# Values of one attention unit and scores of the next in one TensorE burst

## The chip, the cores and the metric

The kernel runs on one core of a Trainium2 chip. The metric is device time in microseconds (us). Three runs of the kernel before took 1695.42, 1698.11 and 1698.41 us; the median is 1698.11.

## The reference

Three steps follow each other; everything is float32.

```
q_c, k_c, v_c = chunks of 64 positions of q, k, v         # 8 x 8 heads, 576 positions, head size 64
scores = (q_c @ k_c^T) / 8
attn   = exp(scores - rowmax); attn = attn / (rowsum + 1e-9)
x      = attn @ v_c                                       # rows: 4608 tokens, columns: 512
h = x @ w_in;   g = h if h > 0 else exp(min(h, 0)) - 1;                        x = g @ w_out
h = x @ w_in2;  g = h if h >= 1, 0 if h <= -1, else (h + 1)^2 / 4;             out = g @ w_out2
```

Both pairs of weights are 512 x 2048 and 2048 x 512.

## The kernel before

Tokens are cut into 9 blocks of 512. A block is made of 4 attention units of 128 tokens, so there are 36 units; a unit is two chunks of 64 tokens for 8 heads. Each factor of the large products is split into a rounded high part and the rest, and three products (high by high, rest by high, high by rest) are added, so a layer of one block takes 16 steps of 12 matmuls into the hidden layer (L603, tile `h`) and 12 out of it (L633, tiles `acc`), all 128 x 512. The steps of the first layer run in the order: block 0's first 7, all of block 1, block 0's other 9, then blocks 2 to 8. What block 0 has summed after its first 7 steps is put aside in DRAM (`part`), loaded again (L845) and added at the end (L867). The second layer, from about 925 us on, has a product scheme of its own (L689, L787) and no attention.

A unit goes through the engines like this. TensorE: scores (`scores`, L429, 16 matmuls of 64 x 64 in the four quarters of the array, tile `s`). VectorE: row maximum (`top`, L443) and subtraction (`sub`, L448). ScalarE: exponential (`exp`, L454). VectorE: sums, guard, reciprocal, product (`total`, `guard`, `invert`, `norm`, L459 to L469). TensorE: four 128 x 128 transposes (`turn`, L474). ScalarE: copy to SBUF (`turned`, L479). TensorE: values (`values`, L481, again 16 matmuls of 64 x 64). ScalarE and VectorE: high part and rest of the result, the x of the first layer (`high`, L499; `low`, L503). From unit 4 on, `s`, the transposes and the values' result `o` take turns in one pair of banks, `a`, which serves one of them at a time.

The order of all instructions is written out by a planner (`Plan`, L37). Every piece of work is an `Op` with an engine (P TensorE, V VectorE, A ScalarE, S the DMA queue of SyncE, X none), a cost, events that it waits for, buffers that it takes and gives. The planner always takes the one that could start first, with a small share of its rank, and so fixes the place of each instruction in its engine's queue; an engine then works strictly in that order. A generator `unit` (L414) yields the Ops of one unit. Buffers that matter: `acc` 2 pairs of banks, `a` 1, `m` 7 slots in SBUF for weights of the second layer on their way to DRAM, for `part` and for results. A unit's x can be written only when the block that used the buffer before is through its hidden layer (`x_free`, L946).

Meanwhile the weights of the second layer are loaded, converted (L194 to L218, L336 to L345), split (L298, L301) and stored (`w3s`, `w4s`, L305).

Of the kernel before, what the change touches and what calls it, by code (L numbers as in the profile page):

```python
# [16 lines left out]
P = 128  # L17
# [86 lines left out]
def chunk_attention_moe_moe2(ctx, tc, qk, v, w1, w2, w3, w4, out):  # L104
# [13 lines left out]
    CH = 64  # L118
# [3 lines left out]
    UPB = BLK // P  # L122
    NU = NT // P
# [22 lines left out]
    T = {}  # L146
# [16 lines left out]
    def pair(tag, i, name):  # L163

        return ps(tag, i, [P, 2, BLK], name)
# [222 lines left out]

    KF = NF - UPB

    def first_loads():
        for g in range(UPB):
            T["qk", g] = wp.tile([P, 2, 4, 2, CH], F32, tag=f"w0_{KF + g}", name=f"qk_{g}")
            if g % 2 == 0:
                v2 = wp.tile([P, 2, 2, 4, D], F32, tag=f"w1_{KF + g // 2}", name=f"v_{g}")
            T["v", g] = v2[:, g % 2]

        def load_qk():
            for i in range(2):
                nc.sync.dma_start(out=T["qk", g][:, i], in_=qk[g, i])  # L400

        def load_v():
            nc.sync.dma_start(out=T["v", g], in_=v[g])

        for i in range(UPB + 1):
            if i < UPB:
                g = i
                yield Op("S", 1.2, load_qk, after=[], event=("qk", g), move=1.46)
            if i >= 1:
                g = i - 1  # L410
                yield Op("S", 0.6, load_v, after=[], event=("v", g), move=0.73)
        yield Op("X", 0.0, lambda: None, after=[], event="weights")

    def unit(u, pool):  # L414
        b, j = divmod(u, UPB)
# [11 lines left out]
            return slice(r * CH, (r + 1) * CH)  # L427

        def scores(i, _):  # L429
            s = T["s", u] = pair(pool, i, ("s2", u))[:, :, :4 * CH].rearrange("p r (t j) -> p r t j", t=4)  # L430
            q, k = T["qk", u][:, 0], T["qk", u][:, 1]
            for t in range(4):
                for r in range(2):
                    for c in range(2):
                        nc.tensor.matmul(  # L435
                            s[half(c), r, t, :], lhsT=q[half(r), t, c, :], rhs=k[half(r), t, c, :],
                            start=True, stop=True,
                        )
# [6 lines left out]
        def sub(i):  # L445

            p = sb("p", i, [P, 4, 2, CH], F32, ("p", u))
            nc.vector.tensor_tensor(  # L448
                out=p.rearrange("p t r j -> p r t j"), in0=T["s", u],
                in1=T["mx", u].to_broadcast([P, 2, 4, CH]), op=ALU.subtract,  # L450
            )
# [28 lines left out]

        def values(i):  # L481

            o = T["o", u] = pair(pool, i, ("o2", u))[:, :, :2 * P].rearrange("p r (s i) -> p r s i", s=2)
            pt, vt = T["pt", u], T["v", u]
            for s in range(2):
                for ch in range(2):
# [21 lines left out]
        if u >= UPB:  # L508
            yield Op("S", 0.6, load_qk, after=before("scores", "q"), event=("qk", u), move=1.46)
            yield Op("S", 0.6, load_v, after=before("values", "v"), event=("v", u), move=0.73)  # L510
        hold = {}

        def scores2(i, k):
            hold["s"], hold["p"] = i, k
            scores(i, k)

        yield Op("P", 1.0, scores2, after=[("qk", u)], take=(pool, "p"), event=("scores", u), late=0.06)
        yield Op("V", 0.6, top)
        yield Op("V", 0.6, lambda: sub(hold["p"]), give=[(pool, hold["s"])])
        yield Op("A", 0.52, exp)  # L520
        yield Op("V", 0.6, total)
        yield Op("V", 0.07, guard)
        yield Op("V", 0.09, invert)
        yield Op("V", 0.6, norm, late=0.1)
        ti, pi = yield Op("P", 0.44, turn, take=(pool, "pt"), give=[("p", hold["p"])], late=0.06)
        yield Op("A", 0.48, lambda: turned(pi), give=[(pool, ti)], event=("pt", u), late=0.1)
        (oi,) = yield Op(
            "P", 1.0, values, after=[("pt", u), ("v", u)] + x_free(b), take=(pool,), give=[("pt", pi)],
            event=("values", u), late=0.06,
# [509 lines left out]
```

## Time and profile before

| | before |
|---|---|
| median of 3 runs | 1698.11 us |
| the profiled execution | 1695.53 us |
| its span | 1693.7 us |
| TensorE busy | 1656.3 us (98%) |
| VectorE busy | 907.2 us (54%) |
| ScalarE busy | 761.8 us (45%) |
| mean granted TensorE clock | 0.993 |

The profiled execution is one of its own, 2.6 us under the median; the span is from its first to its last instruction. PE is TensorE, PEld its weight loads, DVE VectorE, ACT ScalarE, SP SyncE with the DMA queue. Names such as `h<-xh,w` say which tile is written from which. A matmul's length in a row is from its start to its result, and matmuls overlap: twelve of some 0.40 us each follow each other in 2.8 us. What one costs the stream is therefore read from the distance of starts. A 64 x 64 matmul of float32 shows as two records, so a burst of 16 is x32; transposes show as one record each.

### The profile page before, as it was taken

How to read it: one execution, taken by the hardware profiler on the slowest of the kernel's cores; microseconds unless marked ns; L12 is line 12 of the kernel's file. 1: busy time of each engine (PE TensorE's matmuls, PEld its weight loads, DVE VectorE, ACT ScalarE, POOL GpSimd, SP SyncE). 2: the span in 40 equal slices, each digit the busy share in tenths (PEclk: the TensorE clock that was granted, in tenths of full speed). 3: DMA queues.
4: the chain of work that ended last, by engine and by line, in shares of the span. 5: the costliest groups of instructions: out<-in, count | busy, mean ns of one | idle time of the engine just before them, and what ended most of it. 6: DMA issues, size and time to landing. Idle time of an engine off the chain costs nothing.

```text
span 1693.7 us, 26194 instructions
## 1 busy us (share of the span) xinstructions
PE 1656.3 (98%) x10658; PEld 1392.1 (82%) x10658; DVE 907.2 (54%) x1521; ACT 761.8 (45%) x1416; POOL 0.7 (0%) x6
## 2 busy tenths in 40 slices
PE   5999998999999999999999999999999999999998
PEld 4778776777777787778787888888888888888887
DVE  7993455465555645555324464645454545454544
ACT  6883444454444545454433343434343434343433
POOL 0000000000000000000000000000000000000000
PEclk7999999999999999999999999999999999999999
DMA  8640235243332514333355233333333333333332
GB/s 286 204 132 20 63 96 164 71 144 90 110 123 80 172 56 134 94 117 112 107 185 193 100 131 119 127 119 124 120 124 120 125 119 128 119 130 112 112 112 100
DMA packets 105272, 207.23 MB, mean 122 GB/s; under 512 B 8896, under 2 KB 48832, under 8 KB 105152
## 3 DMA queue, kind: packets, MB, share of 16 engines
q1 hardware_dynamic: 105152, 205.56, 36.7%
q8 instruction: 84, 1.38, 0.4%
q14 instruction: 36, 0.29, 0.1%
HBM read 162.53 MB, written 42.99 MB: 121 GB/s over the span
## 4 chain that ended last, share of the span: by engine, by line
PE 87%; DVE 6%; ACT 2%; DMA 1%; issue 0%; SPq 0%; DVEq 0%; ACTq 0%
PE acc L633 23%; PE h L603 21%; PE h L787 11%; PE acc L787 11%; PE acc L689 10%; PE a L689 9%; DVE xu L564 2%; PE a L490 1%; PE a L435 1%; PE a L474 1%; DVE m L218 0%; ACT gh L745 0%; DVE gh L751 0%; DVE t L736 0%; DVE gh L755 0%
## 5 line engine op out<-in xcount | busy, mean ns | idle before, releaser
L633 PE MATMUL acc<-gh,w 128*128 128x512 f32 x1152 | 302.9, 401 | 0.6 <-ACT m L863 0.5
L603 PE MATMUL h<-xh,w 128*128 128x512 f32 x1152 | 293.5, 397 | 1.3 <-DVE t L618 1.3
L603 PEld LDWEIGHTS h<-xh,w 128*128 128x128 f32 x1152 | 217.1, 189 | 53.5 <-DVE t L618 3.0
L633 PEld LDWEIGHTS acc<-gh,w 128*128 128x128 f32 x1152 | 214.0, 189 | 50.7 <-ACT m L863 1.5
L689 PEld LDWEIGHTS a<-xu,w 128*128 128x128 f32 x1512 | 198.8, 188 | 16.4 <-ACT a L721 3.6
L689 PEld LDWEIGHTS acc<-xu,w 128*128 128x128 f32 x1512 | 199.6, 188 | 12.5
L689 PE MATMUL a<-xu,w 128*128 128x256 f32 x1512 | 204.0, 282 | 0.1
L689 PE MATMUL acc<-xu,w 128*128 128x256 f32 x1512 | 203.2, 282 | 0.0
L624 DVE TENSOR_TENSOR gl<-t,gh 128x512 fp32r<-128x512 f32 x144 | 99.1, 688 | 185.7 <-PE acc L633 155.9
L633 PE MATMUL acc<-gl,w 128*128 128x512 f32 x576 | 166.2, 402 | 0.0
L610 ACT ACTIVATE t<-h 128x512 f32<-128x512 f32 x144 | 85.8, 596 | 174.2 <-DVE gl L624 149.4
L618 DVE SCALAR_TENSOR_TENSOR t<-t,h 128x512 f32<-128x512 f32 x144 | 98.7, 685 | 115.4 <-ACT t L614 114.3
L603 PE MATMUL h<-xl,w 128*128 128x512 f32 x576 | 157.3, 395 | 0.0
L603 PEld LDWEIGHTS h<-xl,w 128*128 128x128 f32 x576 | 108.5, 188 | 25.5
L633 PEld LDWEIGHTS acc<-gl,w 128*128 128x128 f32 x576 | 105.3, 189 | 23.2
L621 ACT ACTIVATE gh<-t 128x512 fp32r<-128x512 f32 x144 | 89.9, 625 | 63.5 <-PE acc L633 62.9
L787 PE MATMUL acc<-w,t 128*128 128x512 f32 x432 | 112.7, 397 | 0.4 <-ACT t L759 0.4
L787 PE MATMUL acc<-w,v 128*128 128x512 f32 x432 | 111.7, 394 | 1.4 <-ACT v L759 1.4
L787 PE MATMUL h<-w,p 128*128 128x512 f32 x432 | 112.3, 395 | 0.0
L614 ACT ACTIVATE t<-t 128x512 f32<-128x512 f32 x144 | 90.9, 631 | 4.0
L736 DVE TENSOR_TENSOR t<-acc,z 128x512 f32<-128x512 f32 x36 | 24.9, 691 | 126.2 <-PE acc L689 126.2
L787 PEld LDWEIGHTS acc<-w,v 128*128 128x128 f32 x432 | 76.2, 188 | 14.3 <-ACT v L759 1.6
(99 smaller groups left out, 1772.7 us busy)
## 6 DMA issues: line engine op xcount, KB each, us to landing
w<-w4s SPq DMA_DIRECT2D x144, 512.0 KB, 4.2
raw<-w SPq DMA_DIRECT2D x32, 512.0 KB, 6.4
qk<-qk SPq DMA_DIRECT2D x32, 512.0 KB, 4.0
m<-w SPq DMA_DIRECT2D x64, 256.0 KB, 4.0
w<-w3s SPq DMA_DIRECT2D x28, 512.0 KB, 3.6
w3s<-m SPq DMA_DIRECT2D x48, 256.0 KB, 2.8
v<-v SPq DMA_DIRECT2D x36, 256.0 KB, 2.9
x<-m SPq DMA_DIRECT2D x36, 256.0 KB, 2.9
```

Source lines behind the costliest of these rows:

```text
L435: nc.tensor.matmul(s[half(c), r, t, :], lhsT=q[half(r), t, c, :], rhs=k[half(r), t, c, :], start=True, stop=True,)
L564: nc.vector.tensor_sub(place(j), T[src], T["xh", b, n])
L603: nc.tensor.matmul(h, lhsT=w[:, wi, c, :], rhs=x[:, c, :], start=n == 0, stop=n == 3 * NC_ - 1)
L610: nc.scalar.activation(sb("t", i, [P, BLK], F32, ("act", s)), T["h", s], AF.Relu, scale=-1.0)
L614: nc.scalar.activation(t, t, AF.Exp, scale=-1.0)
L618: nc.vector.scalar_tensor_tensor(out=t, in0=t, scalar=-1.0, in1=T["h", s], op0=ALU.add, op1=ALU.max)
L621: nc.scalar.activation(sb("gh", i, [P, BLK], F32R, ("gh", s)), T["act", s], AF.Copy)
L624: nc.vector.tensor_sub(sb("gl", gi, [P, BLK], F32R, ("gl", s)), T["act", s], T["gh", s])
L633: nc.tensor.matmul(T["acc", 0, b, m], lhsT=w[:, wi, m, :], rhs=T[g, s], start=first and (wi, g) == (0, "gh"), stop=last and g == "gl",)
L689: nc.tensor.matmul(quarter(q), lhsT=w[:, wi, c, :], rhs=x[:, c, :], start=start and k == 0, stop=clean and k == 5, skip_group_check=True,)
L736: nc.vector.tensor_tensor(out=h, in0=halves(hold["h"])[:, 2:4], in1=hold["z"].to_broadcast([P, 2, HB]), op=ALU.add)
L787: nc.tensor.matmul(T["acc", 1, b, 2 * side + k], lhsT=g[:, j, k * P:(k + 1) * P], rhs=w[:, wi], start=(i, j, wi, lo) == (0, 0, 0, False), ...
```

## The change

From the third block on (units 8 and later) a unit's values are no longer an Op of their own: the scores of the next unit take the pair of banks `a`, and its first half of each bank is for the scores, the second half for the values of the unit before, which are issued right ahead of the scores. The copy and the rest of these values (`high`, `low`) are yielded by the next unit too, between its subtraction and its exponential. The pair of banks is given back when both are through. Values lie in the second half of the banks in all units. The planner's cost of scores without values is 0.65 instead of 1.0, of scores with values 1.3.

```diff
+    MERGE = 2 * UPB
         def scores(i, _):
-            s = T["s", u] = pair(pool, i, ("s2", u))[:, :, :4 * CH].rearrange("p r (t j) -> p r t j", t=4)
+            two = T["two", u] if u > MERGE else pair(pool, i, ("s2", u))
+            s = T["s", u] = two[:, :, :4 * CH].rearrange("p r (t j) -> p r t j", t=4)
         def values(i):
-            o = T["o", u] = pair(pool, i, ("o2", u))[:, :, :2 * P].rearrange("p r (s i) -> p r s i", s=2)
+            two = pair(pool, i, ("o2", u))
+            if u >= MERGE:
+                T["two", u + 1] = two
+            o = T["o", u] = two[:, :, 2 * P:].rearrange("p r (s i) -> p r s i", s=2)
...
+        T["unit", u] = values, high, low
+        after = u > MERGE
         def scores2(i, k):
             hold["s"], hold["p"] = i, k
+            if after:
+                T["unit", u - 1][0](i)
             scores(i, k)
-        yield Op("P", 1.0, scores2, after=[("qk", u)], take=(pool, "p"), event=("scores", u), late=0.06)
+        ready, give = [("qk", u)], []
+        if after:
+            ready += [("pt", u - 1), ("v", u - 1)] + x_free((u - 1) // UPB)
+            yield Op("X", 0.0, lambda: None, after=ready)
+            give = [("pt", T["ptslot", u - 1])]
+        yield Op(
+            "P", 1.3 if after else 0.65, scores2, after=ready, take=(pool, "p"), give=give, event=("scores", u), late=0.06
+        )
+        if after:
+            yield Op("X", 0.0, lambda: None, event=("values", u - 1))
         yield Op("V", 0.6, top)
-        yield Op("V", 0.6, lambda: sub(hold["p"]), give=[(pool, hold["s"])])
-        yield Op("A", 0.52, exp)
+        yield Op("V", 0.6, lambda: sub(hold["p"]), give=[] if after else [(pool, hold["s"])], event=("sub", u))
+        if after:
+            yield Op("A", 0.48, T["unit", u - 1][1], after=[("scores", u)], event=("xh", u - 1))
+            yield Op("V", 0.6, T["unit", u - 1][2], after=[("sub", u), ("xh", u - 1)], give=[(pool, hold["s"])], event=("x", u - 1))
+        yield Op("A", 0.52, exp, after=[("sub", u)])
...
+        if MERGE <= u < NU - 1:
+            T["ptslot", u] = pi
+            return
```

TensorE's order around the values of unit 11, before and after. `pt` is a unit's transposed weights, `p` the same before the transposes, `a` the pair of banks.

```order
203 L474 MATMUL a_2072<-ident,p_1983 128x128 x4
204 L633 MATMUL acc_1948<-gl_2013,w_9_1102 128x512 x2
205 L633 MATMUL acc_1949<-gl_2013,w_9_1102 128x512 x2
206 L603 MATMUL h_2083<-xh_241,w_13_1328 128x512 x8
207 L603 MATMUL h_2083<-xl_242,w_13_1328 128x512 x4
208 L633 MATMUL acc_1948<-gh_2056,w_10_1178 128x512 x4
209 L633 MATMUL acc_1949<-gh_2056,w_10_1178 128x512 x4
210 L490 MATMUL a_2112<-pt_2081,v_75 64x64 x16
211 L633 MATMUL acc_1948<-gl_2058,w_10_1178 128x512 x2
212 L633 MATMUL acc_1949<-gl_2058,w_10_1178 128x512 x2
```

In the changed kernel (its lines stand some 2 to 27 further down: L438 is scores, L477 transposes, L496 values, L630 and L660 the large matmuls):

```order
197 L477 MATMUL a_2035<-ident,p_1990 128x128 x4
198 L660 MATMUL acc_1999<-gh_1967,w_8_1036 128x512 x4
199 L660 MATMUL acc_2000<-gh_1967,w_8_1036 128x512 x4
200 L496 MATMUL a_2055<-pt_2048,v_75 64x64 x16
201 L438 MATMUL a_2055<-qk_72 64x64 x16
202 L660 MATMUL acc_1999<-gl_1987,w_8_1036 128x512 x2
203 L660 MATMUL acc_2000<-gl_1987,w_8_1036 128x512 x2
204 L630 MATMUL h_2098<-xh_236,w_13_1334 128x512 x8
205 L630 MATMUL h_2098<-xl_237,w_13_1334 128x512 x4
```

The scores of unit 12 now follow the values of unit 11 at once, into the same `a`; before, they came 24 large matmuls after them. There are 27 such places. Counted in the whole order, 32 to 72 large matmuls, mostly 40 or more, then lie between a burst and the transposes of its unit, except for units 14 (12) and 15 (24).

TensorE at the end of block 0, where the transposes of unit 14 (row 261 before, 260 after) stand ahead of the first output matmuls of block 2 (row 263 in both). Before:

```order
252 L490 MATMUL a_2407<-pt_2405,v_75 64x64 x16
253 L603 MATMUL h_2428<-xh_1729,w_3_550 128x512 x8
254 L603 MATMUL h_2428<-xl_1730,w_3_550 128x512 x4
255 L435 MATMUL a_2444<-qk_72 64x64 x16
256 L603 MATMUL h_2468<-xh_1729,w_4_610 128x512 x8
257 L603 MATMUL h_2468<-xl_1730,w_4_610 128x512 x4
258 L435 MATMUL a_2497<-qk_73 64x64 x16
259 L603 MATMUL h_2521<-xh_1729,w_5_684 128x512 x8
260 L603 MATMUL h_2521<-xl_1730,w_5_684 128x512 x4
261 L474 MATMUL a_2559<-ident,p_2490 128x128 x4
262 L490 MATMUL a_2572<-pt_2567,v_74 64x64 x16
263 L633 MATMUL acc_2595<-gh_2372,w_0_352 128x512 x4
```

After:

```order
254 L660 MATMUL acc_2000<-gh_2337,w_15_1457 128x512 x2
255 L660 MATMUL acc_2000<-gl_2354,w_15_1457 128x512
256 L496 MATMUL a_2454<-pt_2380,v_75 64x64 x16
257 L438 MATMUL a_2454<-qk_72 64x64 x16
258 L630 MATMUL h_2506<-xh_1718,w_5_725 128x512 x8
259 L630 MATMUL h_2506<-xl_1719,w_5_725 128x512 x4
260 L477 MATMUL a_2538<-ident,p_2519 128x128 x4
261 L496 MATMUL a_2547<-pt_2543,v_74 64x64 x16
262 L438 MATMUL a_2547<-qk_73 64x64 x16
263 L660 MATMUL acc_2581<-gh_2382,w_0_371 128x512 x4
```

Two of the three groups of hidden matmuls have moved ahead of block 0's last output matmuls, and the scores of unit 15 have moved behind the transposes of unit 14. VectorE at the same place: the adds of the partial sums (`m<-acc,m`, L867 before, L894 after), the softmax of unit 14 (`p_2490` before, `p_2519` after) and weights of the second layer (L345, L301). Before:

```order
317 L867 TENSOR_TENSOR m_2514<-acc_1948,m_2514 128x512
318 L345 TENSOR_TENSOR m_2539<-m_2539,m_2267 128x256
319 L867 TENSOR_TENSOR m_2518<-acc_1948,m_2518 128x512
320 L867 TENSOR_TENSOR m_2534<-acc_1949,m_2534 128x512
321 L345 TENSOR_TENSOR m_2485<-m_2267,m_2485 128x256
322 L465 RECIPROCAL sm<-sm 128x8
323 L345 TENSOR_TENSOR m_2540<-m_2267,m_2539 128x256
324 L469 TENSOR_TENSOR p_2490<-p_2490,sm 128x512
325 L448 TENSOR_TENSOR p_2556<-a_2497,mx 128x2x4x64
```

After:

```order
316 L446 TENSOR_REDUCE mx<-a_2454 128x8
317 L645 SCALAR_TENSOR_TENSOR t_2494<-t_2494,h_2384 128x512
318 L451 TENSOR_TENSOR p_2519<-a_2454,mx 128x2x4x64
319 L509 TENSOR_TENSOR xl_2328<-a_2454,xh_2327 128x4x128
320 L462 TENSOR_REDUCE sm<-p_2519 128x8
321 L465 TENSOR_SCALAR sm<-sm 128x8
322 L468 RECIPROCAL sm<-sm 128x8
323 L894 TENSOR_TENSOR m_2504<-acc_2000,m_2504 128x512
324 L472 TENSOR_TENSOR p_2519<-p_2519,sm 128x512
325 L301 TENSOR_TENSOR m_2436<-m_2436,m_2534 128x512
326 L894 TENSOR_TENSOR m_2526<-acc_2000,m_2526 128x512
```

Here the third add stands right ahead of the normalising of unit 14 and the fourth behind it; the first two come directly before these rows. On SyncE's queue the load for the third add now comes behind the load of the next `v`, which waits for unit 13's values, and behind the stores of the first two sums; that for the fourth comes behind a further store of weights and a load of `qk`.

ScalarE around the values of unit 12, with the engines that an instruction waits for. Before:

```order
238 L198 ACTIVATE m_2267<-m_2264,bit_bias 128x256
239 L610 ACTIVATE t_2275<-h_2237 128x512 [waits DVE_49,PE_49]
240 L614 ACTIVATE t_2275<-t_2275 128x512 [waits Activation_49]
241 L499 ACTIVATE xh_2301<-a_2280 128x4x128 [waits PE_49]
242 L621 ACTIVATE gh_2319<-t_2222 128x512
243 L610 ACTIVATE t_2331<-h_2306 128x512 [waits DVE_49,PE_49]
```

After:

```order
238 L648 ACTIVATE gh_2273<-t_2192 128x512 [waits PE_49]
239 L637 ACTIVATE t_2318<-h_2213 128x512 [waits DVE_49]
240 L641 ACTIVATE t_2318<-t_2318 128x512 [waits Activation_49]
241 L505 ACTIVATE xh_2327<-a_2275 128x4x128 [waits DVE_49,PE_49]
242 L457 ACTIVATE p_2325<-p_2325 128x512
243 L648 ACTIVATE gh_2337<-t_2230 128x512 [waits PE_49]
```

The copy of the values (`xh`) now waits for VectorE as well as TensorE, and the exponential of the next unit (L457) stands right behind it.

## Rows read from the trace of the kernel before

**Rows 1.** The page, parts 1 and 4: busy time; the chain by engine
```profile
PE 1656.3 (98%) x10658; PEld 1392.1 (82%) x10658; DVE 907.2 (54%) x1521; ACT 761.8 (45%) x1416; POOL 0.7 (0%) x6
...
PE 87%; DVE 6%; ACT 2%; DMA 1%; issue 0%; SPq 0%; DVEq 0%; ACTq 0%
```

**Rows 2.** Stages: stretch, length, busy us (instructions) by engine, granted clock, DMA
```profile
0.00:90.00 90.00, 69.19 (x742) 54.38 (x743) 80.90 (x157) 67.09 (x115) 0.70 (x6) 0.91 0.69 234
90.00:250.00 160.00, 159.47 (x1068) 126.31 (x1068) 87.48 (x152) 81.23 (x141) 0.00 (x0) 1.00 0.24 74
250.00:270.00 20.00, 14.51 (x139) 10.74 (x139) 12.62 (x28) 6.55 (x12) 0.00 (x0) 0.83 0.64 203
270.00:800.00 530.00, 528.72 (x3469) 421.26 (x3462) 290.09 (x520) 265.74 (x499) 0.00 (x0) 1.00 0.35 111
...
915.00:935.00 20.00, 17.20 (x91) 14.32 (x90) 7.16 (x11) 5.45 (x11) 0.00 (x0) 1.00 0.50 158
```

**Rows 3.** Chain of waits, 236 to 275: start, length, what
```profile
236.10 0.62 PE a L435 x32
...
237.86 2.78 PE h L603 x12
...
252.61 4.08 DMA m<-part
```

**Rows 4.** TensorE's timeline around a scores burst: start, length, line, tiles, count
```profile
584.33 1.08 PE L633 MATMUL acc<-gl,w 128*128 128x512 f32 x4
585.33 0.69 PE L435 MATMUL a<-qk 64*64 64x64 f32 x32
585.96 2.13 PE L633 MATMUL acc<-gh,w 128*128 128x512 f32 x8
587.92 1.10 PE L633 MATMUL acc<-gl,w 128*128 128x512 f32 x4
```

**Rows 5.** Inside a values burst: two looks, from the second and the last group
```profile
562.92 0.41 PE L490 MATMUL a<-pt,v 64*64 64x64 f32 x16
...
563.27 0.24 PE L490 MATMUL a<-pt,v 64*64 64x64 f32 x4
```

**Rows 6.** TensorE's timeline at the start: values behind scores, scores alone
```profile
11.89 1.14 PE L435 MATMUL acc<-qk 64*64 64x64 f32 x32
12.80 1.08 PE L490 MATMUL acc<-pt,v 64*64 64x64 f32 x32
...
31.03 1.13 PE L435 MATMUL a<-qk 64*64 64x64 f32 x32 [2.81 <-issue]
32.09 3.31 PE L603 MATMUL h<-xh,w 128*128 128x512 f32 x8
```

**Rows 7.** TensorE's timeline at the end of block 0, idle time in brackets
```profile
251.64 2.13 PE L603 MATMUL h<-xh,w 128*128 128x512 f32 x8
...
259.49 0.63 PE L474 MATMUL a<-ident,p 128*128 128x128 f32 x4 [4.80 <-DVE p L448]
260.81 1.13 PE L490 MATMUL a<-pt,v 64*64 64x64 f32 x32 [0.69 <-ACT pt L479]
261.87 3.97 PE L633 MATMUL acc<-gh,w 128*128 128x512 f32 x8
265.63 1.06 PE L474 MATMUL a<-ident,p 128*128 128x128 f32 x4
```

**Rows 8.** VectorE's timeline: unit 13's maximum and normalising, third add
```profile
236.79 0.69 DVE L443 TENSOR_REDUCE mx<-a 128x8 f32<-128x512 f32 x1 [0.53 <-PE a L435]
...
240.07 0.69 DVE L469 TENSOR_TENSOR p<-p,sm 128x512 f32<-128x512 f32 x1
...
256.72 0.69 DVE L867 TENSOR_TENSOR m<-acc,m 128x512 f32<-128x512 f32 x1 [1.63 <-DMA m<-part]
```

**Rows 9.** ScalarE's timeline: the copy of unit 13's values
```profile
244.56 0.60 ACT L499 ACTIVATE xh<-a 128x512 fp32r<-128x512 f32 x1 [0.26 <-PE a L490]
```

**Rows 10.** TensorE's timeline: the transposes of unit 4
```profile
37.47 0.63 PE L474 MATMUL a<-ident,p 128*128 128x128 f32 x4 [1.14 <-DVE p L448]
```

## The prediction

> **What bounds the kernel now.** I read the page first, then the stages, then TensorE's own timeline. On the page TensorE is busy 98% of the span and makes 87% of the chain that ended last; VectorE, the next engine, is busy 54% [rows 1]. By stage [rows 2] the idle time of TensorE sits in few places: 20.8 us in the first 90 us (90.00 less 69.19), 5.5 us between 250 and 270, 1.3 us in the 530 us from 270 to 800, 2.8 us between 915 and 935. Attention units are worked on up to about 790 us; in that part nearly every microsecond saved on TensorE's own stream is one off the end, and a wait of TensorE costs its full length. So the question is what a burst of small matmuls costs TensorE, not how busy it is.
>
> **What one burst costs.** The large matmuls run at 2.78 us for twelve, 0.232 each [rows 3]. Now look at a burst of scores between them [rows 4]: four large ones start at 584.33 and the burst at 585.33, which is 1.00 us where 4 x 0.232 = 0.93 was due: 0.07 late. From the burst's start to the next large matmul it is 0.63. The eight large ones after it take 587.92 - 585.96 = 1.96 instead of 1.86: another 0.10. The burst as a whole takes 0.07 + 0.63 + 0.10 = 0.80 us off the stream. What of that is work? A burst is 16 small matmuls, recorded as 32 pieces in eight groups of four. In a values burst the second group starts at 562.92 and the eighth at 563.27 [rows 5]: six steps in 0.35, 0.058 each, so eight groups are 0.47 us of work. The other 0.33 is paid for going from the full array to the 64x64 quarters and back.
>
> Is it really paid once when two bursts touch? The start of the kernel has such a pair, at the slow pace [rows 6]: scores at 11.89 are followed by values at 12.80, 0.91 later, while scores with a large matmul behind them take 32.09 - 31.03 = 1.06. The values come without a break.
>
> **The change, part by part.**
>
> *1. Merging.* The order of the changed kernel has 27 places where a values burst (units 8 to 34) is followed at once by the scores of the next unit (9 to 35). Matmuls and weight loads stay as many as before. Two bursts apart cost 2 x 0.80 = 1.60; side by side 0.80 + 0.47 = 1.27. That saves 0.33 each, 27 x 0.33 = 8.9 us. Bounds: if the second burst costs its whole 0.63 and only the edges are shared, 27 x 0.17 = 4.6; if its work is half of the slow pair's 0.91, 0.345 and 9.3. I take 8.9, since rows 5 show the steps themselves.
>
> *2. The stall at the end of block 0.* The order moves a great deal here. Before, [rows 7]: large matmuls start at 251.64, the transposes of unit 14 only at 259.49 after an idle 4.80, values at 260.81, the block's first output matmuls at 261.87, and these eight take 3.76 to the next transposes at 265.63 where 1.86 is due; the stage's granted clock is 0.83, the only one below 1 after the start [rows 2]. From 251.64 to 265.63 are 13.99 us, the work in it is 20 x 0.232 + 0.80 + some 0.4 for the transposes = 5.8, so the stall costs about 8. Its cause is VectorE's queue: an add of the partial sums (L867) waited 1.63 for a load issued at 252.61 that took 4.08 [rows 3, 8], and the normalising of unit 14 and the subtraction of unit 15 stood behind it. In the new order two of the four adds stand ahead of unit 14, and the third one stands right before its normalising. The load for it is issued behind the load of the next v, which waits for the values of unit 13, and behind two stores. With some 0.4 us per issue I put it 1.2 to 1.7 us after these values; it lands 4.1 later, and add and normalising are 2 x 0.69 [rows 8]: 6.7 to 7.2 after the values, 6.2 to 6.7 after the scores beside them. TensorE has only twelve large matmuls (2.8) between, so it waits 3.4 to 3.9 at these transposes, and about 0.8 for the copy of their result: 4.5 of idle. Before, a wait of 4.80 was followed by slow matmuls that cost 1.9 (3.76 less 1.86) and 0.4 more in the values; I give this an even chance and add 1.2. Stall after: 5.7, gain 2.3. Ends: a gain of 5 if the third load is early and only the softmax chain is waited for (about 3 of stall); a loss of 2 if the fourth load, which needs a slot that a store must free first, is last, and the clock falls too.
>
> *3. The softmax chain gets longer.* Scores and values now lie in the same banks, and the order shows that ScalarE's copy of the values waits for VectorE's subtraction, and that the exponential stands behind that copy. Before, for unit 13, scores start at 236.10 and the normalising ends at 240.07 + 0.69 = 240.76: 4.7 us [rows 3, 8]. Now 0.47 of values stand ahead, and a copy of 0.60 [rows 9] within: 5.8 from the burst's start, 7.2 with two other instructions of 0.69 in the way. Save at units 14 (above) and 15 (24 matmuls) at least 32 large matmuls lie between a burst and its transposes: 0.8 + 0.47 + 32 x 0.232 = 8.7. So it hides, with 1.5 us to spare; the cover ends where a chain meets more than two foreign instructions. I put new waits over all units at 1 us, from 0 to 4. The Trainium skill, page PSUM — Partial Sum Buffer, section "PSUM bank collisions raise a hardware error", has the rule against this change: two engines may not touch one bank and quadrant at the same time, other columns or not. The wait in the order agrees with it; no run here shows a collision.
>
> *4. The start.* The planner is told 0.65 instead of 1.0 for scores from the first unit, so the order changes at once: the transposes of unit 4, which wait 1.14 at 37.47 [rows 10], come after one more group of twelve. But this stretch is VectorE's (80.90 busy of 90 [rows 2]), so little of that is kept: a gain of 0.5, from -1 to 2.
>
> Loads: as many as before, in another order on SyncE's queue; priced only in part 2.
>
> **Sum.** 8.9 + 2.3 + 0.5 - 1 = 10.7. The profiled execution took 1695.5 (span 1693.7 and 1.8 around it), so 1684.8. It is 2.6 under the median of the three runs, of which two are at 1698; 1698.1 - 10.7 = 1687.4. I say 1686, some 1.2 over the sum, and give the rivals on the same base (1695.5 + 1.2).
>
> **The rivals.**
>
> *A. The array is drained between the two bursts*, or the second one restarts as after a large matmul: only the edges are shared. For it: the seamless pair was seen at the slow pace only. Against: steps are even within a burst. Saves 4.6 + 1.8 (the other terms) = 6.4: about 1690.
>
> *B. Slower: TensorE waits at the transposes of every merged unit.* In order of place: subtraction, copy of the values, exponential, sums, normalising, then the transposes. It decides against the change once the chain is longer than 8.7 + 0.33 = 9.0 us from the burst's start, 1.8 more than my 7.2, as the 27 waits then eat the 8.9. If a third of them, nine, wait 2 us each, 18 are lost against the forecast: 1704. Against: VectorE has 45% free between 270 and 800, and the old chain took 4.7. The Trainium skill's rule named above is what would bring it about, by the order that it forces between the readers.
>
> *C. The stall at block 0 doubles.* Part loads now wait for values and for stores; if third and fourth follow each other (2 x 4.1 with a store between) at the slow clock, 8 become 16, 10.3 worse than the forecast: 1696, no change.
>
> *D. It does not do what it says*: the bursts are adjacent in the order, but TensorE stops between them for the load of q and k or the copy of the transposes. Two bursts then cost 1.6 again, and 1.8 is left: 1695.
>
> **Chances.** Forecast 0.74, A 0.10, B 0.06, C 0.06, D 0.04. The measurement tells no change from 0.2%, 3.4 us, apart. Faster by more: forecast, A, 0.03 of C and 0.01 of D, 0.88; within: 0.06; slower: 0.06. Range: all good ends together, 9.3 + 5 + 2 = 16.3, give 1679 on the profile's base; the poor ends, 4.6 - 2 - 1 - 4 = -2.4, 1698 to 1700. I keep 1680 to 1694, which leaves out the last corner on both sides and most of B and C.
>
> **What would show it.** In the profile after: values of 32 records followed by scores of 32 records, the first large matmul about 1.10 us after the burst's first piece, not 1.26 (A) or more (D). Idle of TensorE between 270 and 800 about as before, 1 to 3 us; ten or more, at the transposes, is B. Between 250 and 270 one wait of 3 to 4 us at the transposes of unit 14, released by a VectorE instruction behind the add; 8 or more is C. The some 20 merged bursts behind 270 should shorten the way from there to the last values by 6 to 7 us. I am wrong if the time is over 1694, above all if the bursts are merged as I say and the span does not move.

## The result and the profile after

The changed kernel takes 1680.16 us (median of 5 runs, 1678.95 to 1681.81), the kernel before beside it 1698.11; the ratio of the two is 0.9899, with a 95% interval of 0.9886 to 0.9913. The profiled execution took 1680.59 with a span of 1678.8, against 1695.53 and 1693.7 before: 14.9 us less, where the sum said 10.7. The time lies 0.2 us inside the lower end of the range.

First the page of the changed kernel, part 1, in answer to [rows 1]:

```profile
PE 1648.2 (98%) x10658; PEld 1392.4 (83%) x10658; DVE 905.1 (54%) x1521; ACT 756.3 (45%) x1416; POOL 0.7 (0%) x6
```

It has as many instructions as before on each engine, and TensorE is 8 us less busy. Its share of 98% is the old one: the share alone doesn't tell that the kernel got faster, since the edges of a burst count as busy time. Four of the stretches of [rows 2]:

```profile
0.00:90.00 90.00, 72.92 (x748) 57.73 (x749) 80.53 (x156) 67.67 (x116) 0.70 (x6) 0.98 0.70 234
90.00:250.00 160.00, 157.48 (x1069) 126.82 (x1069) 92.85 (x163) 80.82 (x143) 0.00 (x0) 1.00 0.25 82
250.00:270.00 20.00, 19.31 (x141) 15.49 (x141) 13.52 (x26) 11.35 (x22) 0.00 (x0) 0.92 0.72 221
270.00:800.00 530.00, 528.67 (x3508) 424.45 (x3507) 286.21 (x517) 260.61 (x495) 0.00 (x0) 1.00 0.34 108
```

Idle between 270 and 800 is 1.3 us, as before, and 39 more matmul records lie there. The stall of the end of block 0 has shrunk: 0.7 us of idle and a granted clock of 0.92 between 250 and 270, where 5.5 and 0.83 stood; 2.5 us of idle have come in just ahead of 250.

Next, TensorE's timeline around one burst (start, length, line, tiles, count), in answer to [rows 4]:

```profile
354.33 2.11 PE L660 MATMUL acc<-gh,w 128*128 128x512 f32 x8
356.36 0.69 PE L496 MATMUL a<-pt,v 64*64 64x64 f32 x32
356.88 0.65 PE L438 MATMUL a<-qk 64*64 64x64 f32 x32
357.46 1.19 PE L660 MATMUL acc<-gl,w 128*128 128x512 f32 x4
358.49 2.02 PE L660 MATMUL acc<-gh,w 128*128 128x512 f32 x8
```

Values start at 356.36, scores 0.52 later, the next large matmul at 357.46: 1.10 from first piece to large matmul, which is the number that the prediction gave for a merged burst. I then measured every burst of both traces the same way: TensorE's time from the last large matmul ahead of it to the eleventh behind it, less the large ones at 0.232. Before, single bursts of scores and of values take 0.82 each where no wait is beside them; after, 25 of the 26 merged bursts that stand between large matmuls take 1.28 to 1.30 (the 26th runs into the wait shown next). So a merging saves 2 x 0.82 - 1.29 = 0.35, and 27 of them 9.4.

Where TensorE waited between 240 and 800 (line and what it waited for: us, times, longest):

```profile
PE h L630 <- DVE t L645: 3.7, 3, 2.5
PE a L496 <- ACT pt L482: 0.7, 1, 0.7
```

None of it is at transposes (L477). The large matmuls of the first layer (L630) wait for VectorE's step of the activation (L645), which frees their bank. The longest is at the end of block 0, on TensorE's timeline there, in answer to [rows 7]:

```profile
248.88 3.15 PE L630 MATMUL h<-xh,w 128*128 128x512 f32 x8 [2.52 <-DVE t L645]
251.82 1.66 PE L630 MATMUL h<-xl,w 128*128 128x512 f32 x4
253.32 0.60 PE L477 MATMUL a<-ident,p 128*128 128x128 f32 x4
254.61 0.69 PE L496 MATMUL a<-pt,v 64*64 64x64 f32 x32 [0.69 <-ACT pt L482]
```

And what released it, from the chain of waits of the same stretch:

```profile
243.89 1.17 PE acc L660 x5
...
245.08 0.64 ACT gh L648
...
246.35 0.53 DVE m L894
...
246.95 0.68 DVE m L894
247.63 0.60 DVE mx L446
248.23 0.60 DVE t L645
...
248.88 4.61 PE h L630 x12
```

The last output matmuls of block 0 free a buffer, ScalarE can write `gh`, VectorE then does one subtraction, two adds of partial sums (L894) and the row maximum of unit 14, and only then the activation's step for which TensorE waits. But that step had to wait for ScalarE too. Its timeline, and VectorE's normalising of unit 14:

```profile
246.46 0.60 ACT L637 ACTIVATE t<-h 128x512 f32<-128x512 f32 x1 [0.76 <-DVE gl L651]
247.09 0.63 ACT L641 ACTIVATE t<-t 128x512 f32<-128x512 f32 x1
```

```profile
252.40 0.68 DVE L472 TENSOR_TENSOR p<-p,sm 128x512 f32<-128x512 f32 x1
```

L637 starts when the subtraction (`gl`, L651) has freed a `t` buffer, and L641, the last of the activation ahead of VectorE's step, ends at 247.72. VectorE's step starts at 248.2, so its place behind the adds and the maximum makes some 0.4 of the 2.5 us; the rest is the chain through the buffers. The normalising ends at 253.08, 0.24 ahead of the transposes at 253.32: had the large matmuls not waited, TensorE would have stood at the transposes until then. Behind the wait twelve large matmuls take 4.61 instead of 2.79.

The account of the 14.9 us, from the starts of the same large matmuls in the two traces (counted from 0, the 128x256 ones of the second layer too; the 200th: 90.52 and 89.11; the 780th: 237.70 and 233.53; the 900th: 279.55 and 270.19; the 2900th: 787.72 and 773.63; the 3500th: 925.02 and 910.02; the last: 1689.34 and 1674.41). By the 900th the changed kernel has done one values burst less, which is 0.8:

| stretch | gain | mergings x 0.35 | rest | what the rest is |
|---|---|---|---|---|
| to the 200th | 1.4 | 0 | 1.4 | start, another order |
| to the 780th | 2.8 | 5: 1.7 | 1.1 | waits at 107.86 (0.44) and others gone |
| to the 900th | 4.4 | 2: 0.7 | 3.7 | stall at the end of block 0 |
| to the 2900th | 5.5 | 20: 7.0 | -1.5 | two waits of 0.61 at L630 that cost 0.77 each and four delays of 0.06 to 0.21 (2.1 in all), against two waits of 0.65 that cost 0.7 each before: -0.7; 0.8 not assigned |
| to the 3500th | 0.9 | 0 | 0.9 | a wait at 843.31 (0.49) gone |
| to the last | -0.1 | 0 | -0.1 | |

The granted clock of the first 90 us is 0.98 instead of 0.91, but it isn't what is gained at the start: the run weights_late below has 0.89 there and reaches the 200th at 88.88.

### The profile page after: what moved, and what is told of

Its sections match the earlier page's. It is cut to its first block, busy times and chain, and to the rows that moved or that the text cites. A ratio compares the mean times of both kernels' runs of the same rounds, so it can differ in the third digit from the quotient of the medians.

```text
span 1678.8 us, 26192 instructions
## 1 busy us (share of the span) xinstructions
PE 1648.2 (98%) x10658; PEld 1392.4 (83%) x10658; DVE 905.1 (54%) x1521; ACT 756.3 (45%) x1416; POOL 0.7 (0%) x6
## 4 chain that ended last, share of the span: by engine, by line
PE 91%; DVE 6%; ACT 2%; issue 0%; DMA 0%; SPq 0%; ACTq 0%
PE acc L660 24%; PE h L630 24%; PE h L814 11%; PE acc L814 11%; PE acc L716 10%; PE a L716 9%; DVE xu L591 2%; PE a L496 1%; PE a L438 1%; PE a L477 1%; ACT gh L772 0%; DVE gh L778 0%; DVE t L763 0%; DVE gh L782 0%; ACT gh L786 0%
## 5 line engine op out<-in xcount | busy, mean ns | idle before, releaser
L660 PE MATMUL acc<-gh,w 128*128 128x512 f32 x1152 | 301.2, 399 | 2.0 <-ACT gh L648 1.9
L630 PE MATMUL h<-xh,w 128*128 128x512 f32 x1152 | 295.1, 398 | 3.8 <-DVE t L645 3.7
L630 PEld LDWEIGHTS h<-xh,w 128*128 128x128 f32 x1152 | 217.6, 190 | 57.1 <-DVE t L645 6.3
L660 PEld LDWEIGHTS acc<-gh,w 128*128 128x128 f32 x1152 | 213.9, 189 | 51.2 <-ACT gh L648 2.1
L651 DVE TENSOR_TENSOR gl<-t,gh 128x512 fp32r<-128x512 f32 x144 | 99.3, 690 | 216.2 <-PE acc L660 196.4
L637 ACT ACTIVATE t<-h 128x512 f32<-128x512 f32 x144 | 85.8, 596 | 202.5 <-DVE gl L651 194.1
L660 PE MATMUL acc<-gl,w 128*128 128x512 f32 x576 | 164.8, 399 | 0.0
L630 PE MATMUL h<-xl,w 128*128 128x512 f32 x576 | 158.1, 396 | 0.0
L645 DVE SCALAR_TENSOR_TENSOR t<-t,h 128x512 f32<-128x512 f32 x144 | 98.6, 685 | 100.0 <-ACT t L641 99.4
L630 PEld LDWEIGHTS h<-xl,w 128*128 128x128 f32 x576 | 109.4, 190 | 26.0
L660 PEld LDWEIGHTS acc<-gl,w 128*128 128x128 f32 x576 | 106.8, 189 | 24.4
L641 ACT ACTIVATE t<-t 128x512 f32<-128x512 f32 x144 | 90.8, 631 | 3.5
```

Of the source, the lines that this page charges most:

```text
L630: nc.tensor.matmul(h, lhsT=w[:, wi, c, :], rhs=x[:, c, :], start=n == 0, stop=n == 3 * NC_ - 1)
L637: nc.scalar.activation(sb("t", i, [P, BLK], F32, ("act", s)), T["h", s], AF.Relu, scale=-1.0)
L641: nc.scalar.activation(t, t, AF.Exp, scale=-1.0)
L645: nc.vector.scalar_tensor_tensor(out=t, in0=t, scalar=-1.0, in1=T["h", s], op0=ALU.add, op1=ALU.max)
L651: nc.vector.tensor_sub(sb("gl", gi, [P, BLK], F32R, ("gl", s)), T["act", s], T["gh", s])
L660: nc.tensor.matmul(T["acc", 0, b, m], lhsT=w[:, wi, m, :], rhs=T[g, s], start=first and (wi, g) == (0, "gh"), stop=last and g == "gl",)
```

## The experiments

Theory E is the prediction's: the gain is the edges of the bursts, 0.33 each. Its rivals were O (it is the new order, which the planner makes from the new costs), C (the longer softmax chain has no spare), and for the stall V (VectorE's adds) and L (the loads of partial sums). Theory Q came up on the way: VectorE's in-order queue. These letters are the experiments' own; C is rival B of the prediction. The kernel before took 1694.7 to 1695.8 beside these runs, and 1698.1 beside the changed kernel (medians), so I compare ratios and the spans of the profiled executions; the changed kernel's span is 1678.8.

**cost_only: the planner's cost alone.** The kernel before, nothing merged.

```diff
-        yield Op("P", 1.0, scores2, after=[("qk", u)], take=(pool, "p"), event=("scores", u), late=0.06)
+        yield Op("P", 0.65, scores2, after=[("qk", u)], take=(pool, "p"), event=("scores", u), late=0.06)
```

> The kernel before with one number changed: the planner is told 0.65 instead of 1.0 for scores. No burst is merged; the order up to the scores of unit 8 becomes that of the changed kernel, and the end of block 0 keeps the old order. Theory E (each of the 27 merges saves 0.33 us of TensorE because the way into and out of the quarter array is paid once): only the start's 1.4 us can come, so 1694 to 1697, no change. Rival O (the gain is made by the new order that the cost numbers bring, and the merging is beside the point): at least half of the 15 us between the two profiled executions, 1688 or less.

Measured: 1690.99 against 1695.81, ratio 0.9972 (0.9963 to 0.9982), 4.7 us off the span of the profiled execution. That is more than E allowed and less than the half that O wanted. 2.4 of it are gained by the 200th large matmul, 1.1 up to the 780th, 1.2 at the stall, where TensorE still waits at the transposes of unit 14 for the subtraction of unit 15, as it did before. Waits from 240 to 800:

```profile
PE a L474 <- DVE p L448: 4.1, 1, 4.1
```

So the order that the other cost makes gives about a third as much as the whole change, without any merging. How much of it is left in the changed kernel isn't shown: no run merges with the old cost.

**from16: merged from the fifth block on**, 19 places.

```diff
-    MERGE = 2 * UPB
+    MERGE = 4 * UPB
```

> The changed kernel with merging from unit 16 on instead of 8: 19 merged bursts instead of 27, the end of block 0 in the old order. Theory E: 19 x 0.33 = 6.3 plus 1.4 at the start, 7.7 under the kernel before: 1688 on the base of its profiled execution, and a stall at the end of block 0 of about 8 us as before. Rival S (most of the gain is the stall at the end of block 0 and the start, the merges give little): 1693 or more.

Measured: 1685.87, ratio 0.9943 (0.9927 to 0.996). Its span is 5.3 us under that of cost_only. 19 x 0.35 = 6.6; it loses 1.0 at the start and 0.5 at the stall, whose wait stands at the transposes as before (4.5). With these two put back, a merged place gives 0.36 here too.

**between and ahead: one small full-array matmul**, in all 27 merged bursts. In between it stands after the values and ahead of the scores, in ahead it stands ahead of the values. Work and order are the same but for its place; the line is that of between, in ahead it writes to the same place by `T["two", u + 1]`.

```diff
+                nc.tensor.matmul(T["two", u][:, 0, :CH], lhsT=ident, rhs=ident[:, :CH], start=True, stop=True)
```

> The changed kernel with one small matmul on the full array (128 x 128 by 64 columns of the identity, into the place that the scores then overwrite) between the values and the scores of each of the 27 merged bursts. The order is the same otherwise. Theory E: the full array is entered and left once more in each, so the 0.33 come back 27 times, 8.9 us, beside the matmul's own 0.1 to 0.2: 11 to 14 us over the changed kernel, and each burst 1.5 to 1.7 us from its first piece to the next large matmul instead of 1.09. Rival O (order, not edges): only the matmul's own cost, 3 to 5 us.

> The changed kernel with the same small matmul on the full array placed ahead of the values, behind the large matmuls, in each of the 27 merged bursts: the array stays whole there, so it costs only itself. Control of the run with the matmul between. Theory E: 27 x 0.1 to 0.2, 3 to 5 us over the changed kernel, and 8 to 9 us under the run with the matmul between. Rival O: the same as the run with the matmul between, within 2 us.

Measured: between 1693.44, ratio 0.9985 (0.9976 to 0.9994); ahead 1686.01, ratio 0.9944 (0.9929 to 0.9958). TensorE's timeline at the same burst, first of between:

```profile
359.32 2.10 PE L661 MATMUL acc<-gh,w 128*128 128x512 f32 x8
361.36 0.69 PE L496 MATMUL a<-pt,v 64*64 64x64 f32 x32
361.98 0.44 PE L526 MATMUL a<-ident 128*128 128x64 f32 x2
362.35 0.69 PE L438 MATMUL a<-qk 64*64 64x64 f32 x32
362.97 1.19 PE L661 MATMUL acc<-gl,w 128*128 128x512 f32 x4
364.00 2.02 PE L661 MATMUL acc<-gh,w 128*128 128x512 f32 x8
```

then of ahead:

```profile
357.30 2.11 PE L661 MATMUL acc<-gh,w 128*128 128x512 f32 x8
359.25 0.33 PE L489 MATMUL a<-ident 128*128 128x64 f32 x2
359.51 0.69 PE L497 MATMUL a<-pt,v 64*64 64x64 f32 x32
360.02 0.65 PE L438 MATMUL a<-qk 64*64 64x64 f32 x32
360.60 1.19 PE L661 MATMUL acc<-gl,w 128*128 128x512 f32 x4
361.63 2.02 PE L661 MATMUL acc<-gh,w 128*128 128x512 f32 x8
```

From the eight large matmuls to the next eight: 4.68 in between, 4.33 in ahead, 4.16 without the matmul. Measured as above, the median burst takes 1.82, 1.46 and 1.29. The same instruction costs 0.17 where the array goes over to its quarters anyway, and 0.53 where it must come back for it: 0.36 more, which is the 0.35 that a merging saves. E had said 11 to 14 us and 3 to 5 over the changed kernel; the spans are 13.1 and 5.3 over. They differ by 7.8 us, less than 27 x 0.36 = 9.7, since ahead comes 0.8 later out of the start and 0.6 hides at the end of block 0; 0.5 is not assigned. This shows that the edges are paid for, and that the seam between values and scores has none. The Trainium skill, page TensorEngine Tiling (Array Packing), section "Key Properties", says that a change of tiling mode drains TensorE; the 0.36 agrees with it, though a trace doesn't show the draining itself.

**plus2 and plus4: a longer chain.** The row maximum of merged units is done three or five times; its result is the same. Each extra one makes VectorE's chain from scores to transposes 0.6 longer.

```diff
+            for _ in range(2 if u > MERGE else 0):
+                nc.vector.tensor_reduce(out=mx[:, :, :, 0], in_=T["s", u], op=ALU.max, axis=AX.X)
```

> The changed kernel with VectorE's row maximum done three times instead of once in each of the 27 merged units (the same result): 2 x 0.69 = 1.4 us more in every softmax chain, the order of all else unchanged. Theory E with a spare of 1.5 us per unit: nearly all of it hides, at most 2 us over the changed kernel, mostly at the end of block 0. Rival B (the longer chain already has no spare): 27 x 1 us and more, 20 us or more over it, with TensorE idle at the transposes.

> The same with the maximum done five times: 2.8 us more in each chain. Where 32 large matmuls lie between burst and transposes (four units) 1.2 us are not covered, where 40 or more lie nothing is missing: 5 us, and 2 to 3 at the end of block 0, so 5 to 9 us over the changed kernel, waits of TensorE at those transposes only. Rival B: 27 x 2.5, some 60 us.

Measured: plus2 1701.08, ratio 1.0039 (1.0024 to 1.0054); plus4 1747.2, ratio 1.0308 (1.0291 to 1.0325). By the time E failed in both, and C's sums were met: 1.2 us of a chain that was to have 1.5 to spare cost 20 in the span, and 2.4 us cost 66. But the waits are not where C had them. From 240 to 800, plus2:

```profile
PE h L632 <- DVE t L647: 15.5, 15, 4.0
PE a L479 <- DVE p L474: 1.3, 2, 1.0
```

plus4:

```profile
PE h L632 <- DVE t L647: 42.8, 21, 5.4
PE a L479 <- DVE p L474: 2.7, 2, 2.4
```

The transposes (L479) wait 1.3 and 2.7 in all, even with 2.4 us more in the chain. It is the first layer's large matmuls (L632) that wait, for the activation's step (L647), which has nothing to do with the softmax and only stands behind it in VectorE's queue. One such place in plus2, a wait of 1.29 that ends at 351.34:

```profile
347.43 0.63 ACT L643 ACTIVATE t<-t 128x512 f32<-128x512 f32 x1
348.07 1.42 DVE L448 TENSOR_REDUCE mx<-a 128x8 f32<-128x512 f32 x2
350.61 0.68 DVE L647 SCALAR_TENSOR_TENSOR t<-t,h 128x512 f32<-128x512 f32 x1
```

What L647 needs from ScalarE (L643) is there at 348.06; the two added maxima (L448), a rounding and a copy come first. That gave theory Q.

**plus2_known: the same work as plus2, told to the planner.**

```diff
-        yield Op("V", 0.6, top)
+        yield Op("V", 1.8 if after else 0.6, top)
```

> The row maximum is done three times in merged units, as in plus2 (20 us slower than the changed kernel), but the planner is told 1.8 instead of 0.6 for it and so orders VectorE's queue by it. Theory Q (the loss of plus2 came from VectorE's in-order queue, in which the added maxima held up the activation's step that large matmuls wait for): with the order made for it most of the 20 us come back, under 8 us over the changed kernel, about 1684 to 1688, and the wait of the large matmuls of ff_in on VectorE falls from 18 us to under 8. Rival C (the longer softmax chain itself has no spare): told or not, TensorE waits; at least 15 us over, 1695 or more, with the wait moved to the transposes.

Measured: 1683.13, ratio 0.9925 (0.991 to 0.994). 18 of the 20 us come back with not one instruction less. From 240 to 800:

```profile
PE h L632 <- DVE t L647: 3.2, 6, 1.2
PE a L479 <- DVE p L474: 0.8, 1, 0.8
```

15.5 has become 3.2. So Q holds for most of the loss, and C is out: there is room for the work, but not in an order that was made without it.

**adds_late and weights_late: other work out of VectorE's way at the end of block 0.** The first holds the adds of the partial sums back until two more groups are through, the second starts the second layer's weights later.

```diff
-            yield Op("V", 0.6, add, after=[ready, ("part", m)], give=give)
+            yield Op("V", 0.6, add, after=[ready, ("part", m), ("g", SPLIT + 2 * NF - 4)], give=give)
```

```diff
-    S2 = 2 * NF
+    S2 = 2 * NF + 4
```

> The changed kernel with one event more before the four adds of block 0's partial sums: they stand behind VectorE's part of the activation of the fourth step of block 2, for which TensorE waits 2.5 us in the changed kernel. Theory V (VectorE's order alone makes that stall): the wait falls to under 1 us, the clock does not fall behind it, 3 us under the changed kernel. Rival L (the load for the fourth add lands at 255.1 and holds the first output matmuls of block 2 in any case): TensorE waits there instead, at most 1 us is won.

> The changed kernel with the second layer's weights begun four steps later, so that buffers are free for all four loads of the partial sums at once; the four adds stand together ahead of the softmax of unit 14, and 24 large matmuls instead of 12 between its scores and its transposes. Theory L: with the loads early, the stall at the end of block 0, 4.9 us in the changed kernel, falls to 1 to 2: 3 us or more under the changed kernel. Theory V: the four adds stand ahead of the activation that TensorE waits for, so the wait there stays 2 us or grows, and at most 1 us is won.

Measured: 1679.4, ratio 0.9908 (0.9893 to 0.9923), and 1680.74, ratio 0.9915 (0.99 to 0.993): neither differs from the changed kernel (0.9899). In adds_late 2.1 us of wait remain at L630 and 0.5 comes in at the transposes, so the two adds alone did not decide (V), nor did a wait at the output matmuls take over (L). The edit does not free VectorE's queue there, though: the subtraction of unit 14 (L451, at 246.35) now stands ahead of the activation's step where the adds stood. In weights_late the wait moves to where an add frees an accumulator; from 240 to 800:

```profile
PE h L630 <- DVE t L645: 2.1, 3, 1.2
PE acc L660 <- DVE m L894: 2.0, 1, 2.0
```

**t3: a third buffer for the activation's inputs.** In the rows above, VectorE's step must wait for ScalarE, and ScalarE (L637) for a `t` buffer that the step before it frees late.

```diff
-BUFS = dict(m=7, p=2, pt=1, t=2, g=2, h=2, a=1, acc=2, q=2, v=2, ld=6, xs=4, xu=16, t2=2, g2=4, z=2, hh=2, ol=1, om=1)
+BUFS = dict(m=7, p=2, pt=1, t=3, g=2, h=2, a=1, acc=2, q=2, v=2, ld=6, xs=4, xu=16, t2=2, g2=4, z=2, hh=2, ol=1, om=1)
```

> A third buffer for the activation's input copies (t), nothing else; the planner moves what it moves by that. Theory Q (the wait of 2.5 us at the first large matmul of ff_in behind block 0 comes from the activation's chain, which waits for a t buffer that the step before frees late): that wait goes, stall at the end of block 0 falls from 4.9 to about 2 us, and the single waits of 0.6 at ff_in too: 3 to 4 us under the changed kernel, about 1677. Rival L (the loads of partial sums decide there): another wait of 2 us or more stands between 245 and 270, and the time stays within 1.5 us of the changed kernel.

Measured: 1677.45, ratio 0.9889 (0.9872 to 0.9905). The stretch from 250 to 270, then the waits from 240 to 800:

```profile
250.00:270.00 20.00, 19.43 (x145) 15.40 (x144) 14.32 (x28) 11.71 (x23) 0.00 (x0) 1.00 0.69 220
```

```profile
PE h L630 <- DVE t L645: 1.2, 2, 0.6
```

The wait of 2.5 is two of 0.6 now, the clock stays at 1.00, and from the 780th to the 900th large matmul 3.2 us are gained over the changed kernel (4.1 less some 0.9 for two groups of transposes that t3 does outside this stretch); the start comes out 1.2 later. So the stall goes with the third buffer and the order that the planner makes for it, and the loads did not decide. The two are not parted: this order also puts 36 large matmuls instead of 12 between the burst and the transposes of unit 14. By the rows of the changed kernel the buffer alone would have left TensorE to wait there for the normalising. In total time its interval overlaps with the changed kernel's; that it is the faster of the two is likely and not settled.

**from4: merged from the second block on**, 31 places.

```diff
-    MERGE = 2 * UPB
+    MERGE = UPB
```

> Merged from the second block on (31 bursts instead of 27, four more in the stage up to 90 us). Theory E (each merging saves 0.33 us of TensorE's stream wherever TensorE is the bound): the four lie where VectorE is the bound, so they give 0 to 1.3 us, and the chain that is longer there can cost as much: within 2 us of the changed kernel, 1678.5 to 1682. Rival C (the longer chain is exposed where VectorE is busy): transposes of units 5 to 8 wait 1 us or more each, 3 us or more slower, 1683 or more.

Measured: 1719.58, ratio 1.0137 (1.0122 to 1.0152), 36 us more in the span than the changed kernel. E failed by far; C has the side right and the place wrong, since the waits at transposes are at most 3.1 us (one that the changed kernel has too), and 1.5 where it has none. It is one single wait. TensorE's timeline:

```profile
79.13 0.69 PE L496 MATMUL a<-pt,v 64*64 64x64 f32 x32
79.64 0.65 PE L438 MATMUL a<-qk 64*64 64x64 f32 x32
116.04 1.22 PE L630 MATMUL h<-xh,w 128*128 128x512 f32 x2 [35.75 <-ACT xh L505]
```

VectorE's before its end:

```profile
113.29 0.68 DVE L218 SCALAR_TENSOR_TENSOR m<-m,m 128x512 uint32<-128x512 uint32 x1
113.89 0.68 DVE L446 TENSOR_REDUCE mx<-a 128x8 f32<-128x512 f32 x1
114.60 0.69 DVE L451 TENSOR_TENSOR p<-a,mx 128x512 f32<-128x512 f32 x1
```

and ScalarE's:

```profile
115.39 0.60 ACT L505 ACTIVATE xh<-a 128x512 fp32r<-128x512 f32 x1 [0.70 <-DVE p L451]
```

The values of unit 7, the last of block 1, stand in the banks with the scores of unit 8. Their copy (L505) waits for the subtraction of unit 8 (L451), which reads the same banks, and this unit belongs to block 2 and is in no hurry: its maximum stands behind the weights' rounding (L205 to L252) on VectorE, which runs until 113.9. Block 1's large matmuls need unit 7. So this is what merging costs where it costs: a unit's values can't leave before the next unit's softmax has begun. In the changed kernel units 7 and 8 are not merged, and behind them VectorE has room.

**t3_true: t3, and the planner's costs scaled to measured ones.**

```diff
-            cost = op.cost * (2 if op.eng == "P" and t < COLD else 1)
+            cost = op.cost * {"P": 1.07, "V": 1.14, "A": 1.17}.get(op.eng, 1) * (2 if op.eng == "P" and t < COLD else 1)
```

> The third t buffer of t3 (1677.45), and the planner's costs scaled to what the traces show: TensorE's times 1.07, VectorE's times 1.14, ScalarE's times 1.17 (TensorE's from 0.232 measured to the planner's figure, VectorE's 0.60 against what it is told). Theory Q (what is left of waits comes from orders in which VectorE's queue is longer than the planner believes): the waits of ff_in on VectorE, 1.2 us in t3, go, and those of the start (VectorE is the bound there) shrink: 1 to 4 us under t3, 1673.5 to 1676.5. Rival (the order at the start, which changes most here, is a matter of luck): the first 200 large matmuls end 2 us or more later or earlier than in t3, and the total follows that and nothing else.

Measured: 1695.82 against 1695.44, ratio 1.0001 (0.9992 to 1.001). Q's forecast failed, and the rival is right only in its first half: the 200th large matmul comes 2.0 later than in t3 (92.34 against 90.33), another 2.9 are lost up to the 3500th, and 11.1 in the last stage, which no one had thought of. Waits from 905 to the end, t3_true:

```profile
PE acc L814 <- ACT v L786: 11.1, 8, 1.4
```

In t3 there is one such wait of 1.4, here there are eight. Durations nearer to the measured ones did not make a better order.

## Why the prediction was right, and where it was not

The change gains for the reason forecast, the edges of the bursts. That the time lies inside the range is in part luck: it is inside by 0.2 us, and two of the five runs are below 1680. All four terms came out better than said, so their errors add up.

**What bounds the kernel** was read rightly: microseconds off TensorE's stream between 90 and 800 came off the end, nearly all of them.

**1. Merging: 8.9 said, 9.4 measured (25 places read, taken for all 27).** The step rests on two values read from [rows 4, 5], 0.80 for a burst and 0.47 for the work in it; they are 0.82 and 0.47 (1.29 less 0.82). Rows of the slow pace [rows 6] had the seam right: values and scores follow each other without a break. The runs between and ahead show that it is the edge (0.36). Rivals A and D are out: 1.10 to the next large matmul, not 1.26.

**2. The stall: gain of 2.3 said, 3.7 measured; the wait stood elsewhere.** I had TensorE wait 3.4 to 3.9 at the transposes of unit 14 for the third add and its load. The third add found its load landed; only the fourth waited (1.42), and nothing on the path stood behind it. TensorE waits 2.5 at the large matmuls ahead of the transposes, for the activation's step. The failed step is "the third one stands right before its normalising ... lands 4.1 later": I followed the load alone and not the activation, whose chain through `gh`, `gl` and the `t` buffer holds the large matmuls ahead of the transposes (2.5), with some 0.4 of it from the adds and the maximum in VectorE's queue. The wait at the transposes was not wrong in itself but covered: the normalising ended 7.9 us after the values (6.7 to 7.2 said), 0.24 ahead of the transposes. My 3.4 to 3.9 also left out the 0.5 that the scores themselves take. That slow matmuls would follow was given even odds, and they did (4.61 less 2.79). Rival C, the doubled stall, is out.

**3. The longer chain: -1 said (0 to -4); about -0.7 from waits behind the 900th, but the reason for it did not hold.** "1.5 us to spare" counts only the way to the transposes. Of that spare no run showed the end: with 0.6 x 4 = 2.4 us more in plus4 the transposes wait 2.7 in all, though there the large matmuls ahead of them have waited already. What has no spare is the activation's step behind the chain on the same in-order engine. The statement that the cover ends "where a chain meets more than two foreign instructions" looked at it from the wrong side: the chain is itself what foreign instructions meet. The price is the order's, as plus2 and plus2_known show (20 us against 3). What the shared banks alone force, which the prediction named as a wait and priced at nothing but chain length, is from4's 35.7 us. The rule of the Trainium skill that the prediction cites (page PSUM — Partial Sum Buffer, section "PSUM bank collisions raise a hardware error") would have such a wait; no run shows a collision, or that the rule is why the order has it.

**4. The start and the order: 0.5 said, 1.4 at the start, 1.1 up to the 780th, 0.9 near the end.** Undersized: cost_only alone gives 4.7. I priced the order at one place, though the planner uses the cost at every unit. Why 0.65 makes the better order isn't shown: with its edges a burst takes 0.82, as far from 0.65 as from 1.0.

The four make 9.4 + 3.7 - 0.7 + 3.4 = 15.8, of which 0.9 is not found again in the 14.9; the sum had 10.7. The 20 merged bursts behind 270, for which I had 6 to 7 us, gave 7.0, and 5.5 with the waits and what isn't assigned. The forecast was 5.8 over the measured median: 4.2 from the sum (0.5 + 1.4 + 0.3 + 2.9 - 0.9), 1.2 that I added for the median, and 0.4 by which the profiled execution lies over its own.

## What to carry to other kernels

Count what a small burst costs from the large instruction ahead of it to the one behind it, not by its own length; two bursts of the same tile shape side by side then save one pair of edges. Look for the price in other places than the merged work: who reads the shared banks, in which order, and whose result is now bound to whose. On an in-order engine the spare of a chain is not the spare of what stands behind it, so when work on it grows, tell whatever makes the order, and look at each stage again, since an order that is good in one stage can lose more in another.

## What the runs showed that was not expected

- One full-array matmul of 128x64 costs 0.17 us ahead of a burst of quarters and 0.53 inside it.
- A single idle stretch of 2.52 us on TensorE was followed by slow matmuls: the next twelve large ones took 4.61 us instead of 2.79, with a granted clock of 0.55 between 251.0 and 253.3 (0.92 between 250 and 270). In weights_late a wait of 2.0 was followed by a drop too (0.93 in the same stretch). The two waits of 0.6 in t3 were not; there it is 1.00.
- Fixed orders are fragile: 1.2 us more work per unit on an engine that is 54% busy cost 20 us, and 3 once the order knew of it.
